# Weight slices 64 bytes further apart in SBUF, and x and g buffers at other distances modulo 512

## The chip, the cores and the metric

The kernel runs on one core of a Trainium2 chip. A core has a matrix engine (TensorE, PE in the profile, its weight loads PEld), a vector engine (VectorE, DVE), a scalar engine (ScalarE, ACT), GpSimd (POOL) and a queue engine (SyncE, SP) that issues the transfers (DMA) between main memory and the on-chip memory SBUF. SBUF has 128 partitions; an address below is a byte offset within a partition. TensorE reads both operands from SBUF (the weights, which it loads first, and the moving rows, which stream past them) and writes sums to PSUM. The metric is device time in microseconds, lower is better.

## What is computed

A linear attention with decaying state, and a feed-forward network on its output:

```python
for t in range(S):                       # S = 768, B, H, D = 4, 8, 48
    kt, vt, rt = (k[:, :, t], v[:, :, t], r[:, :, t])
    cur = np.einsum('bhd,bhe->bhde', u[None] * kt, vt)
    y[:, :, t] = np.einsum('bhd,bhde->bhe', rt, state + cur)
    state = w[None, :, :, None] * state + np.einsum('bhd,bhe->bhde', kt, vt)
x = np.ascontiguousarray(y.transpose(0, 2, 1, 3)).reshape(B * S, H * D)   # 3072 x 384
h = x @ w_in                             # 384 x 2048
g = h * np.clip(h + 3.0, 0.0, 6.0) / 6.0
return g @ w_out                         # 2048 x 384
```

All inputs and the output are float32.

## The kernel before

The attention is done in 24 half steps of 64 tokens (`attention`, small matmuls of L319). It leaves its output in the x buffers. The feed-forward network goes over 6 groups g of 512 tokens and, in each, over 16 slices f of 128 hidden units, 96 units in all. One unit is:

- `ffn1`: nine matmuls by `hidden` (L128) make h, 128 hidden units by 512 tokens. Three parts (weights high by x high, weights low by x high, weights high by x low: the table `PARTS`) times three blocks j of 128 rows of w_in. The high and low parts are a split of each float32 number in two, so that the fast matmul format (F32R) keeps enough digits.
- ACT takes relu(h + 3) to t (L388), DVE takes min(t, 6) times h (L390), ACT writes the high part of g (L394), DVE the low part (L183).
- `ffn2`: nine matmuls by `project` (L135) add g to three output sums o, with the same three parts times three blocks m.

Every one of the 18 matmuls has weights of its own, 128 x 128, taken from `w_hi` or `w_lo`, and moving rows of 512 elements, taken from x (L128) or g (L135). `ffn2` of a unit follows `ffn1` of the next one, so on TensorE groups of nine alternate: h of unit n+1, o of unit n, and so on. The order on every engine is made ahead of time: operations are recorded with estimated costs (class `Schedule`), a list scheduler sorts them, and the result is emitted as it stands. The estimates know sizes and engines, and no addresses.

During the first group of tokens the weights come in: `weights(f)` loads slice f of `wcat` into `raw[f % 2]` (L200), and ACT and DVE make from it `w_hi[:, f]` (L219 or L220) and `w_lo[:, f]` (L183). Where the schedule has TensorE idle, dummy matmuls on `ident` (L490) fill in.

The tiles that matter here, in the order in which they lie in SBUF: a reserve of 16384 bytes for descriptors of transfers that GpSimd issues (this kernel has none of those), four constants of 32 bytes, `w_hi` and `w_lo` of 16 slices each (one slice has 2 x 384 elements, 3072 bytes: w_in's part, then w_out's), the attention's tiles, x0 and x1 (16384 bytes each, used in turn by groups g), t0 and t1, g0, g1 and g2 (4096 bytes each, used in turn by units), `raw`, `z`, `cv`. A tile begins where the one before it ends. 3072, 4096, 16384 and 2048 (a t buffer) are multiples of 512, so all weight slices lie at one place modulo 512, and all x and g buffers at another.

Of the kernel before, what the change touches and what calls it, by code (L numbers as in the profile page):

```python
# [9 lines left out]
F32R = mybir.dt.float32r  # L10
# [12 lines left out]
DM, DFF = H * D, 2048  # L23
NF = DFF // 128
NG = NSTEP // 2

W_MIN, W_MAX = 0.5, 2.0

# [108 lines left out]
def fast_path(tc, mp, pp, sb, w_hi, w_lo, b3, wm, badi, hps, ops3, rT, kT, rt, kt, vt, wp, wu, wcat, out):  # L139
    nc = tc.nc  # L140
# [4 lines left out]
    def two(name, shape, dt=F32):  # L145
        return [sb(f"{name}{q}", shape, dt, mp) for q in range(2)]

    def one(name, shape, dt=F32):
        return sb(name, shape, dt, mp)
# [10 lines left out]
    PQ, IW = E[:, 0:8], E[:, 8:16, 1:C + 1]  # L160


    xt = two("x", [128, 2, 4, 2, 256], F32R)
    tt = two("t", [128, 512])
    gg = [one(f"g{q}", [128, 2, 512], F32R) for q in range(3)]
    mask = one("mask", [128, C], U8)
    NW = 2 * DM
    raw, z = two("raw", [128, NW], I64), two("z", [128, NW])
# [286 lines left out]
    for n, u in enumerate(units):  # L455
        g, f, c0, ns = u
# [26 lines left out]
    for (_, free, _, _), (start, _, _, _) in zip(pe, pe[1:]):  # L483
        n = int((start - free - 0.2) / 0.22)
# [14 lines left out]
def rwkv_ffn_kernel(ctx: ExitStack, tc: tile.TileContext, rT, kT, rt, kt, vt, wp, wu, wcat, ys, out):  # L499
    nc = tc.nc  # L500
# [3 lines left out]
    def sb(name, shape, dt=F32, pool=cp):  # L504
        return pool.tile(shape, dt, name=name)

    w_hi = sb("w_hi", [128, NF, 2, DM], F32R)
    w_lo = sb("w_lo", [128, NF, 2, DM], F32R)
    b3 = sb("b3", [128, 1])
    wm = sb("wm", [1, 4])  # L510
    badi = sb("badi", [1, 1], I32)
# [4 lines left out]
    with tc.tile_pool(name="main", bufs=1) as mp, tc.manual_schedule():  # L516
        fast_path(tc, mp, pp, sb, w_hi, w_lo, b3, wm, badi, hps, ops3, rT, kT, rt, kt, vt, wp, wu, wcat, out)
# [3 lines left out]
    with tc.If(bad != 0):  # L521
        with tc.tile_pool(name="fb", bufs=1) as fb, tc.tile_pool(name="fl", bufs=1) as fl:
# [11 lines left out]
            with tc.For_i(0, NSTEP, 1) as st:  # L534
                a = [fl.tile([128, C, D], F32, tag=f"a{n}", name=f"a{n}") for n in range(2)]
# [32 lines left out]
            with tc.For_i(0, NG, 1) as g:  # L568
                xf = fb.tile([128, 3, 512], F32, name="xf")
                x = fb.tile([128, 3, 2, 512], F32R, name="xr")  # L570
# [7 lines left out]
                for f in range(NF):  # L578
                    h, t, gt = hps[f % 2], fl.tile([128, 512], F32, tag="t", name="ft"), fl.tile(
                        [128, 2, 512], F32R, tag="gg", name="fg")  # L580
# [72 lines left out]
```

## Time and profile before

| | us |
|---|---|
| median of 3 runs | 521.6 |
| lowest and highest of them | 518.52, 525.86 |
| span of the profiled execution, first to last instruction | 520.5 |

The profile is of one execution of its own; its span is its time, and stands 1.1 us below the median of the three runs. Three stages can be seen in the table of stretches, whose columns are the length, each engine's busy time with its number of instructions, the granted clock of TensorE (1.00 is full), the share of the DMA engines and GB/s:

```profile
0.00:48.60 48.60, 43.20 (x842) 40.39 (x843) 40.00 (x64) 15.77 (x21) 17.93 (x22) 1.00 0.79 230
48.60:135.00 86.40, 81.83 (x1000) 64.83 (x1000) 78.32 (x106) 47.62 (x70) 23.93 (x17) 0.98 0.45 146
135.00:508.00 373.00, 372.68 (x3344) 301.28 (x3343) 178.05 (x279) 124.59 (x199) 38.11 (x35) 1.00 0.18 53
508.00:520.50 12.50, 3.96 (x22) 2.78 (x20) 1.38 (x2) 1.78 (x3) 0.00 (x0) 0.74 0.19 69
```

Up to 48.6 us the first half steps of the attention run and the first weights come in; up to 135 us the first 16 units run beside the rest of the weights; then come the other 80 units with the attention between them, and a tail of 12.5 us in which the last sums are written out. In the third row TensorE is busy for 372.68 of 373.00 us.

### The profile page before, as it was taken

To read this page: it belongs to the slowest core of one execution; us is meant where nothing else is said; L and a number is where in the kernel's file an instruction comes from. 1 tells how busy PE (TensorE), PEld (TensorE's weight loads), DVE (VectorE), ACT (ScalarE), POOL (GpSimd) and SP (SyncE) were. 2 spreads that over 40 slices of the span, in tenths; PEclk is the share of its full clock that TensorE was granted. 3 is DMA by queue.
4 is the path that set the end of the run, shared out by engine and by line. 5 is a ranking of instruction groups with operands and counts; after the bars stand their busy time and mean duration, and the time that the engine had idled before them with its cause. 6 is when DMAs were issued, how large, how long until landed. Compare 5 with 4: busy or idle time off the path is not lost.

```text
span 520.5 us, 11985 instructions
## 1 busy us (share of the span) xinstructions
PE 501.7 (96%) x5204; PEld 409.3 (79%) x5204; DVE 297.8 (57%) x449; ACT 189.8 (36%) x291; POOL 80.0 (15%) x73
## 2 busy tenths in 40 slices
PE   8799799999999999999999999999999999999993
PEld 8789587886888877888778888778888878888882
DVE  6899889979833477533576433577333463333331
ACT  1334667652433332333332333332433323333331
POOL 2253013244300122000231000231000220000000
PEclk9999899999999999999999999999999999999997
DMA  8976535452500153200254200253100110100001
GB/s 223 292 232 182 171 131 191 151 159 66 158 3 0 33 150 118 85 2 0 68 157 117 79 0 1 67 164 112 63 0 1 49 35 15 62 0 1 0 1 66
DMA packets 22909, 44.31 MB, mean 85 GB/s; under 512 B 3649, under 2 KB 11970, under 8 KB 22850
## 3 DMA queue, kind: packets, MB, share of 16 engines
q1 hardware_dynamic: 22850, 43.47, 27.3%
q8 instruction: 43, 0.70, 0.6%
q14 instruction: 16, 0.13, 0.1%
HBM read 36.38 MB, written 4.72 MB: 79 GB/s over the span
## 4 chain that ended last, share of the span: by engine, by line
PE 87%; DVE 5%; DMA 3%; SPq 1%; ACT 1%; issue 1%; DVEq 0%; ACTq 0%
PE o L135 38%; PE h L128 37%; PE PP L319 9%; DMA raw<-wcat 3%; PE h L490 2%; PE U L319 1%; DVE w_lo L183 1%; SPq L193 1%; DVE z L215 1%; DMA kt<-kt 1%; SPq L370 1%; DVE cv L213 1%; DVE z L183 0%; DVE g L183 0%; PE o L319 0%
## 5 line engine op out<-in xcount | busy, mean ns | idle before, releaser
L135 PE MATMUL o<-g,w_hi 128*128 128x512 f32 x576 | 199.3, 400 | 4.8 <-ACT g L394 3.2
L128 PE MATMUL h<-x,w_hi 128*128 128x512 f32 x576 | 165.2, 395 | 0.4 <-DVE w_hi L220 0.4
L390 DVE SCALAR_TENSOR_TENSOR t<-t,h 128x512 f32<-128x512 f32 x96 | 65.9, 686 | 132.3 <-ACT t L388 132.1
L135 PEld LDWEIGHTS o<-g,w_hi 128*128 128x128 f32 x576 | 108.6, 189 | 32.5 <-ACT g L394 3.7
L388 ACT ACTIVATE t<-h,b 128x512 f32<-128x512 f32 x96 | 66.1, 688 | 182.4 <-PE h L128 182.3
L128 PEld LDWEIGHTS h<-x,w_hi 128*128 128x128 f32 x576 | 106.7, 188 | 24.2 <-DVE w_hi L220 0.8
L135 PE MATMUL o<-g,w_lo 128*128 128x512 f32 x288 | 113.4, 394 | 0.0
L183 DVE TENSOR_TENSOR g<-t,g 128x512 fp32r<-128x512 f32 x96 | 70.2, 732 | 36.1 <-ACT g L394 35.9
L394 ACT CAST g<-t 128x512 fp32r<-128x512 f32 x96 | 59.5, 620 | 65.8 <-DVE t L390 65.8
L128 PE MATMUL h<-x,w_lo 128*128 128x512 f32 x288 | 81.7, 392 | 0.0
L128 PEld LDWEIGHTS h<-x,w_lo 128*128 128x128 f32 x288 | 54.0, 188 | 12.4 <-DVE w_lo L183 0.5
L135 PEld LDWEIGHTS o<-g,w_lo 128*128 128x128 f32 x288 | 54.4, 189 | 10.8
L183 POOL TENSOR_TENSOR ks<-kT,E 112x512 f32<-112x512 f32 x22 | 28.1, 1278 | 224.4 <-PE PP L319 163.3
L319 PE MATMUL U<-V,KH 64*48 64x48 f32 x704 | 40.0, 204 | 0.6 <-issue 0.6
L183 POOL TENSOR_TENSOR KH<-kt,TW 128x384 f32<-128x384 f32 x21 | 21.7, 1035 | 97.2 <-PE U L319 68.9
L319 PEld LDWEIGHTS U<-V,KH 64*48 64x48 f32 x704 | 34.5, 121 | 0.7 <-issue 0.7
L490 PE MATMUL h<-ident 128*128 128x128 f32 x236 | 29.2, 280 | 0.0
L490 PEld LDWEIGHTS h<-ident 128*128 128x128 f32 x236 | 27.6, 193 | 0.7
L319 PEld LDWEIGHTS PP<-X,V 64*48 64x48 f32 x736 | 18.1, 119 | 11.2 <-DVE X L351 4.2
L319 PEld LDWEIGHTS PP<-RP,ks 48*64 48x64 f32 x736 | 19.7, 132 | 7.6 <-issue 6.8
L319 PE MATMUL PP<-X,V 64*48 64x64 f32 x736 | 21.5, 227 | 3.4 <-DVE X L351 3.4
L362 ACT CAST x<-PP 112x512 fp32r<-112x512 f32 x23 | 13.5, 586 | 29.5 <-PE U L319 29.5
(77 smaller groups left out, 337.4 us busy)
## 6 DMA issues: line engine op xcount, KB each, us to landing
raw<-wcat SPq DMA_DIRECT2D x16, 768.0 KB, 4.7
kT<-kT SPq DMA_DIRECT2D x24, 224.0 KB, 3.0
rT<-rT SPq DMA_DIRECT2D x24, 224.0 KB, 3.4
kt<-kt SPq DMA_DIRECT2D x24, 192.0 KB, 3.0
V<-vt SPq DMA_DIRECT2D x24, 192.0 KB, 3.0
rt<-rt SPq DMA_DIRECT2D x16, 192.0 KB, 2.7
outT<-cv SPq DMA_DIRECT2D x12, 256.0 KB, 2.2
x<-x SPq DMA_DIRECT2D x72, 32.0 KB, 2.0
```

Source lines behind the costliest of these rows:

```text
L128: nc.tensor.matmul(h, (w_hi, w_lo)[wl][:, f, 0, 128 * j:128 * j + 128], x(j, hl), start=(m == 0 and j == 0), stop=(m == 2 and j == 2))
L135: nc.tensor.matmul(o[m], (w_hi, w_lo)[wl][:, f, 1, 128 * m:128 * m + 128], g(hl), start=(clear and k == 0), stop=(f == NF - 1 and k == 2), ...
L183: emit = lambda e: eng[e].tensor_tensor(out=out, in0=in0, in1=in1, op=op)
L193: S.add({"sp": cost}, [], [(name, q)], lambda e, dst=dst, src=src: dma(dst[q], src[i]), LEAD)
L213: S.add({"dve": 0.56}, [kr], [("cv", 1)], lambda e: dve.tensor_scalar(out=sg, in0=up_i, scalar1=-2 ** 31, scalar2=None, op0=ALU.bitwise_an ...
L215: S.add({"dve": 0.95}, [kz, ("cv", 1)], [kz], lambda e: dve.scalar_tensor_tensor(out=zi, in0=zi, scalar=3, in1=sg, op0=ALU.logical_shift_l ...
L319: nc.tensor.matmul(out, lhsT, rhs, start=start, stop=True, skip_group_check=True)
L362: S.add({"act": 0.59}, keys, [kx + (0,)], lambda e: act.copy(out=hi, in_=yt), LEAD)
L388: S.add({"act": 0.23 + 0.23 * ns}, [("h", n % 2), "b3"], [kt_], lambda e: act.activation(out=t[:, :T], in_=h[:, :T], func=AF.Relu, bias=b3 ...
L390: last = S.add({"dve": 0.13 + 0.28 * ns}, [("h", n % 2), kt_], [kt_], lambda e: dve.scalar_tensor_tensor(out=t[:, :T], in0=t[:, :T], scala ...
L394: S.add({"act": 0.18 + 0.22 * ns}, [kt_], [kg + (0,)], lambda e: act.copy(out=gt[:, 0, :T], in_=t[:, :T]))
L490: nc.tensor.matmul(hps[1][:, :128], ident, ident, start=True, stop=True)
```

## The change

The diff moves tiles in SBUF. On each engine the same instructions stand in the same order with the same shapes; only addresses differ.

```diff
+STEP = 16
+X_AT, G_AT = (0, 8), (0, 8, 4)
...
-    xt = two("x", [128, 2, 4, 2, 256], F32R)
+    def moved(name, n, at):
+        return one(name, [128, n + 8], F32R)[:, at:at + n]
+
+    xt = [moved(f"x{q}", 2 * 4 * 2 * 256, a).rearrange("p (c j l t) -> p c j l t", c=2, j=4, l=2)
+          for q, a in enumerate(X_AT)]
     tt = two("t", [128, 512])
-    gg = [one(f"g{q}", [128, 2, 512], F32R) for q in range(3)]
+    gg = [moved(f"g{q}", 2 * 512, a).rearrange("p (l t) -> p l t", l=2) for q, a in enumerate(G_AT)]
...
-    w_hi = sb("w_hi", [128, NF, 2, DM], F32R)
-    w_lo = sb("w_lo", [128, NF, 2, DM], F32R)
+    w_hi, w_lo = (sb(name, [128, NF, 2 * DM + STEP], F32R)[:, :, 0:2 * DM].rearrange("p f (a m) -> p f a m", a=2)
+                  for name in ("w_hi", "w_lo"))
...
-    nc = bacc.Bacc("TRN2", target_bir_lowering=False, num_devices=1)
+    nc = bacc.Bacc("TRN2", target_bir_lowering=False, num_devices=1, dynamic_dma_scratch_size=4096)
```

Each weight slice is followed by 16 unused elements (64 bytes), so slice f lies 64 f bytes further on. Each x and g buffer has 8 elements (32 bytes) more than it needs, and begins 0, 8 or 4 elements into its tile. The reserve at the start of SBUF shrinks from 16384 to 4096 bytes, which makes room. The addresses that follow:

| | bytes modulo 512, before | after |
|---|---|---|
| slice f of w_hi and of w_lo | 128 | (128 + 64 f) modulo 512 |
| x0, x1 | 192, 192 | 192, 256 |
| g0, g1, g2 | 192, 192, 192 | 256, 320, 336 |
| t0, t1 | 192, 192 | 256, 256 |
| raw0, raw1 (modulo 256) | 0, 0 | 160, 160 |

Before, the moving rows lie 64 bytes behind the weights, modulo 512, for every pair. After it, the distance is 64 - 64 f for x0, 128 - 64 f for x1 and g0, 192 - 64 f for g1 and 208 - 64 f for g2. So each buffer meets eight different distances as f goes from 0 to 15.

## The prediction, made before the changed kernel was run

> **What bounds the kernel now.** I read the page first: the span, the busy shares, the granted clock and the chain of work that ended last.
>
> ```profile
> span 520.5 us, 11985 instructions
> PE 501.7 (96%) x5204; PEld 409.3 (79%) x5204; DVE 297.8 (57%) x449; ACT 189.8 (36%) x291; POOL 80.0 (15%) x73
> PE 87%; DVE 5%; DMA 3%; SPq 1%; ACT 1%; issue 1%; DVEq 0%; ACTq 0%
> PE o L135 38%; PE h L128 37%; PE PP L319 9%; DMA raw<-wcat 3%; PE h L490 2%; PE U L319 1%; DVE w_lo L183 1%; SPq L193 1%; DVE z L215 1%; DMA kt<-kt 1%; SPq L370 1%; DVE cv L213 1%; DVE z L183 0%; DVE g L183 0%; PE o L319 0%
> ```
>
> TensorE is the bound, and by the chain's second line it is two lines of code: L128 (h from x and the weights) and L135 (o from g and the weights), 37% and 38%, together some 390 us of 520.5. The groups say how many instructions that is: 576 with `w_hi` and 288 with `w_lo` on each line, 1728 in all.
>
> ```profile
> L135 PE MATMUL o<-g,w_hi 128*128 128x512 f32 x576 | 199.3, 400 | 4.8 <-ACT g L394 3.2
> L128 PE MATMUL h<-x,w_hi 128*128 128x512 f32 x576 | 165.2, 395 | 0.4 <-DVE w_hi L220 0.4
> L135 PEld LDWEIGHTS o<-g,w_hi 128*128 128x128 f32 x576 | 108.6, 189 | 32.5 <-ACT g L394 3.7
> ```
>
> Their mean of 400 or 395 ns is not the pace, since matmuls overlap. The pace is read from the timeline in the last, undisturbed part (columns: start, length, engine, line, operands, count).
>
> ```profile
> 454.76 0.85 PE L128 MATMUL h<-x,w_hi 128*128 128x512 f32 x3
> 455.22 0.65 PEld L128 LDWEIGHTS h<-x,w_lo 128*128 128x128 f32 x3
> 455.45 0.85 PE L128 MATMUL h<-x,w_lo 128*128 128x512 f32 x3
> 456.13 0.85 PE L128 MATMUL h<-x,w_hi 128*128 128x512 f32 x3
> 457.05 0.39 PE L135 MATMUL o<-g,w_lo 128*128 128x512 f32 x1
> 457.05 0.42 PEld L135 LDWEIGHTS o<-g,w_hi 128*128 128x128 f32 x2
> 457.08 0.69 ACT L388 ACTIVATE t<-h,b 128x512 f32<-128x512 f32 x1 [2.06 <-PE h L128]
> 458.88 0.62 PE L128 MATMUL h<-x,w_hi 128*128 128x512 f32 x2
> 459.18 0.69 DVE L183 TENSOR_TENSOR g<-t,g 128x512 fp32r<-128x512 f32 x1 [0.69 <-ACT g L394]
> ```
>
> From 454.76 to 458.88 are 18 matmuls, nine of L128 and nine of L135: 4.12 us, 228.9 ns each, and 1728 x 228.9 = 395.5 us. That is the whole of the chain's 75% (390 us), so nearly every nanosecond won or lost per matmul counts in full. The rows show a second thing: each weight load starts with the matmul before the one that it serves (457.05 and 457.05). Two reads of SBUF by TensorE run side by side, and the change alters the distance between just these.
>
> **Is there something to win?** In one short stretch TensorE had half its clock.
>
> ```profile
> 57.30:59.60 2.30, 2.30 (x6) 1.82 (x7) 2.27 (x4) 1.69 (x3) 0.00 (x0) 0.50 0.08 12
> 58.31 0.63 PE L135 MATMUL o<-g,w_lo 128*128 128x512 f32 x1
> 58.74 1.05 PE L135 MATMUL o<-g,w_hi 128*128 128x512 f32 x2
> 59.59 0.56 PE L135 MATMUL o<-g,w_lo 128*128 128x512 f32 x1
> ```
>
> The first row is the table of stretches (its 0.50 is the granted clock). Three steps from 58.31 to 59.59 are 1.28 us, 427 ns each. Half of that, 213 ns, is what the same matmul would take at full clock if nothing else limited it. It takes 228.9. So some 15.6 ns of each matmul at full clock are not streaming, 1728 x 15.6 = 27 us in all. If these come from the weight load and the moving rows meeting in SBUF, the change can touch them: before, all weight slices lie at 128 modulo 512 bytes and all x and g buffers at 192, one distance (64) for every pair. After it, slices step through eight positions and the buffers lie at 192, 256, 256, 320 and 336.
>
> The trace has a test of that. Where the attention's matmuls follow, the last matmul of a group of L128 has no weight load beside it, because the next load comes late.
>
> ```profile
> 249.63 0.65 PEld L128 LDWEIGHTS h<-x,w_hi 128*128 128x128 f32 x3
> 249.86 0.85 PE L128 MATMUL h<-x,w_hi 128*128 128x512 f32 x3
> 250.64 0.21 PEld L319 LDWEIGHTS PP<-RP,ks 48*64 48x64 f32 x8 [0.36 <-issue]
> 250.81 0.69 ACT L388 ACTIVATE t<-h,b 128x512 f32<-128x512 f32 x1 [2.06 <-PE h L128]
> 245.74 0.85 PE L128 MATMUL h<-x,w_hi 128*128 128x512 f32 x3
> 246.20 0.19 PEld L135 LDWEIGHTS o<-g,w_hi 128*128 128x128 f32 x1
> 246.68 0.69 ACT L388 ACTIVATE t<-h,b 128x512 f32<-128x512 f32 x1 [2.05 <-PE h L128]
> ```
>
> In the upper four rows the third matmul starts at about 250.31 and the next weight load only at 250.64; in the lower three the load for L135 starts at 246.20 with the third matmul. ACT, which waits for that matmul, starts 0.95 us after the three began in the first case and 0.94 us in the second. Without a load beside it the matmul is not sooner done; if the load took 15 ns from it, the first figure would be the smaller. So the 15.6 ns are not shown to come from the load, and the distance between the two reads should not matter. Nor do other engines' accesses show: in the fence of 454.76 ACT and DVE read and write t and g during the run, and the 4.12 us hold.
>
> **The change, part by part.**
>
> *Weight slices 64 bytes further apart (L128, L135).* No instruction is added or moved. Per matmul the price is bounded by -15.6 ns (the row at half clock) and, upward, by a weight load that loses its cover:
>
> ```profile
> 108.07 0.50 PE L135 MATMUL o<-g,w_hi 128*128 128x512 f32 x1
> 108.17 0.19 PEld L135 LDWEIGHTS o<-g,w_lo 128*128 128x128 f32 x1
> 108.41 0.40 PE L135 MATMUL o<-g,w_lo 128*128 128x512 f32 x1
> ```
>
> Here the load came 0.10 us late and the next matmul started 0.34 us after the last instead of 0.23: +110 ns. Between -15.6 and +110 I take 0, since the nearest rows are those with and without a load, 0.94 and 0.95. What hides a somewhat slower load is the matmul beside it: a load takes 189 ns of the 229 (the mean in the groups' third row), so some 40 ns are free.
>
> *x and g at other offsets.* ACT and DVE write and read the same elements. The chain h, t, g that must be done before L135 starts on it: h ends at 456.98, ACT starts at 457.08, DVE's last step ends at 459.18 + 0.69 = 459.87, and the group of L135 that reads it comes after the nine matmuls from 458.88, at 458.88 + 2.06 = 460.94. So 1.07 us hide a slower write of g or x. I take 0. Were that cover gone, each further 0.1 us would cost 96 x 0.1 = 9.6 us; at four instructions of some 0.7 us it would take each of them over a third longer.
>
> *The reserve of 4096 instead of 16384 bytes, and all tiles after it.* No queue of GpSimd issues a transfer in this kernel, so the reserve itself costs nothing. But the tiles behind it shift: `raw` lay at a multiple of 256 bytes and now lies 160 past one (32 past a multiple of 64); kT, rT, V, kt and rt lie 32 past a multiple of 64 before and after. `raw` takes in the weights, and some of its landings are waited for:
>
> ```profile
> raw<-wcat SPq DMA_DIRECT2D x16, 768.0 KB, 4.7
> kT<-kT SPq DMA_DIRECT2D x24, 224.0 KB, 3.0
> L200 SPq DMA_DIRECT2D raw<-wcat x16: 327/328/1492, 5.1 to 103.3; - x16
> ACT z L210 <- DMA raw<-wcat: 5.2, 3, 2.5
> ACT cv L212 <- DMA raw<-wcat: 4.3, 1, 4.3
> DVE z L211 <- DMA raw<-wcat: 2.8, 1, 2.8
> ```
>
> Five waits, 12.3 us. Bounds: at best nothing changes; at worst `raw` moves at the rate of kT (224 KB in 3.0 us, 75 KB per us), 10.3 us instead of 4.7, which over five waits is +28 us. I take 0. The smaller transfer takes 3.0 us for under a third of the bytes, so most of a landing isn't bytes, and kT's rate is the size's doing far more than the position's.
>
> A rule of the Trainium skill speaks against the change here: "DMA: Bandwidth & Descriptors", section "How a descriptor splits into AXI transactions", says that a descriptor which doesn't start at a multiple of 256 bytes fetches from the boundary below. By it, as an estimate, a row of 6144 bytes at 160 past a boundary needs 197 beats instead of 192, 2.6% more, 0.12 us of 4.7, and the sum would have 0.6 us over five waits in place of 0. No run here shows which of the two ends of a transfer it concerns.
>
> **The sum.** Own time of the profiled execution 520.5 us; L128 and L135 0; ACT and DVE 0; DMA 0: 520.5. The median of the runs shown, 521.6, is 1.1 above that span, so the forecast is 521.6 us: no change. The runs shown of before differ among themselves by 7.3 us (518.52 to 525.86), and a measurement of this kernel can't tell less than about 2%, 10.4 us, from no change.
>
> **Rivals.**
>
> *The two reads do meet, and spreading them frees seven of eight pairs (faster).* For it speaks that the 15.6 ns are absent at half clock, where reads have twice the time; against it, that the matmul without a load beside it is as long. At 7/8 of 15.6 ns, 1728 matmuls give 23.6 us: 498 us. At half, 13.5 us: 508 us. It decides (10.4 us) from 6 ns per matmul. The Trainium skill ("TensorE: Matmul & The Clock Gate", section "Back-to-back issue gap") has N / 2.4 + 2.5 ns at full clock, 216 ns for 512 columns. By it, as an estimate, 1728 x 13 = 22.5 us would be there to win, 499 us; the trace shows 228.9 and no matmul at 216.
>
> *At one distance in eight a weight load loses its cover (slower).* Then 1728 / 8 = 216 matmuls pay 110 ns: +23.8 us, 546 us. It decides from 95 matmuls, one in 18, and needs a load over 40 ns longer than its 189. Against it: loads of both lines and both tables show 0.19 us everywhere at full clock. For it: only one distance was ever seen.
>
> *`raw` lands later (slower).* It decides when each of the five waited-for landings comes 2.1 us later, 6.8 instead of 4.7 us; at the upper bound the time is 550 us. Against it: it is 16 loads, the last issued at 103 us, and eleven of them land unwaited for.
>
> *The change does what it says and nothing comes of it* is the forecast itself.
>
> **How the numbers follow.** No change 0.78; the reads meet (faster by over 2%) 0.12; a load loses its cover 0.06; `raw` 0.04. Hence faster 0.12, same 0.78, slower 0.10. The likeliest case's own range is the spread of the runs with a microsecond on either side, 517 to 527. Reaching down to the half-size gain (508, with a microsecond for the spread: 507) and up to 528 leaves out the full gain, both slower cases and a tail: some 0.18.
>
> **What would show it.** Right: 18 matmuls still take 4.12 us in undisturbed stretches of every weight slice, for x0 and x1 and all three g, loads stay at 0.19, and `raw` lands in 4.7. The faster rival would show as a pace that changes with the slice, near 3.9 us per 18 for most and 4.12 for a few; the slower one as steps of 0.34 us at the same slices in every group, or as longer loads; the `raw` one as longer landings and longer waits before L210 to L212, all before 120 us. If the pace differs by slice at all, my reading of the matmul without a load beside it was wrong.

## The result: 0.6% slower, and a pace that now changes from slice to slice

The median of 20 runs is 526.05 us against 522.36 us before (20 runs). The ratio is 1.0064 with a 95% interval of 1.0042 to 1.0086: slower, by some 3.3 us. The ratio compares fast executions alone and leaves out two slow ones of the changed kernel (530.63 and 531.67 us), so it is a little smaller than that of the two medians. The loss is far inside the 2% that the forecast took for no change, but it is clear of zero, and the forecast had nothing that would cause it.

The page of the changed kernel hardly shows it (L132 is the old L128, L139 the old L135).

```profile
span 521.4 us, 11993 instructions
PE 504.3 (97%) x5204; PEld 409.1 (78%) x5204; DVE 297.6 (57%) x449; ACT 189.8 (36%) x291; POOL 82.0 (16%) x73
PE o L139 38%; PE h L132 38%; PE PP L327 8%; DMA raw<-wcat 2%; PE h L498 2%; PE U L327 1%; DMA kt<-kt 1%; DVE w_lo L191 1%; DVE z L223 1%; DVE z L191 1%; SPq L201 1%; DVE cv L221 1%; DVE X L359 1%; DVE g L191 0%; PE o L327 0%
L139 PE MATMUL o<-g,w_hi 128*128 128x512 f32 x576 | 199.3, 400 | 4.1 <-ACT g L402 2.3
L132 PE MATMUL h<-x,w_hi 128*128 128x512 f32 x576 | 166.4, 397 | 0.4 <-DVE w_hi L228 0.4
```

The chain is the same, TensorE is as busy, and the mean length of a matmul, 400 and 397 ns, is what it was to within 2 ns. The page's span is only 0.9 us longer, because one execution's start-up differs from the next by more than the effect: the first matmul of the second group of tokens begins at 132.96 us here and at 135.01 in the profile of before (131.8 to 140.7 over all the profiles below). The answer stands in the timeline. Two groups of nine matmuls of L132, from undisturbed stretches of the same page:

```profile
455.50 0.86 PE L132 MATMUL h<-x,w_hi 128*128 128x512 f32 x3
456.20 0.86 PE L132 MATMUL h<-x,w_lo 128*128 128x512 f32 x3
456.90 0.86 PE L132 MATMUL h<-x,w_hi 128*128 128x512 f32 x3
457.60 0.39 PE L139 MATMUL o<-g,w_hi 128*128 128x512 f32 x1
...
501.41 0.84 PE L132 MATMUL h<-x,w_hi 128*128 128x512 f32 x3
502.09 0.84 PE L132 MATMUL h<-x,w_lo 128*128 128x512 f32 x3
502.77 0.84 PE L132 MATMUL h<-x,w_hi 128*128 128x512 f32 x3
503.44 0.39 PE L139 MATMUL o<-g,w_hi 128*128 128x512 f32 x1
```

The first group (slice 3) takes 2.10 us for nine steps, 233 ns each; the second (slice 14) 2.03 us, 226 ns each. Before, an undisturbed group took 2.06. From the first matmul of L132 in unit 16 to that in unit 95 there are 372.54 us here and 369.19 before: +3.35 us, which is the loss. Of the 1422 steps from one matmul of the two lines to the next, 67 are over 260 ns long (the attention lies in between, or a group starts late) and take 58.90 us against 58.72 before. The other 1355, called undisturbed below, take 313.64 us against 310.47: +3.2 us, 2.3 ns each. So the loss is in the pace and not in the gaps.

From here on a pace is worked out from the starts of the matmuls in the trace: the mean of the last six of the eight steps within a group of nine, over all groups that no attention interrupts. Sorted by the distance of the moving rows from the weights, modulo 256 bytes, the changed kernel gives, for L132 and for L139 at the distances that are multiples of 64:

| distance | L132, ns | L139, ns |
|---|---|---|
| 0 | 229.0 (single groups 226.7 to 231.5) | 228.9 (227.3 to 231.5) |
| 64 (all pairs before: 228.9) | 229.3 (228.8 to 231.0) | 230.5 (228.8 to 233.3) |
| 128 | 232.7 | 232.8 |
| 192 | 233.3 | 233.3 |

The two buffers x0 and x1 meet a given distance at different slices and agree within 0.7 ns in the mean. Nothing of the rest of the change shows: `raw` lands in 4.6 us (4.7 before), and its waits are no longer than they were (4.9, 2.6 and 1.4 us against 5.2, 4.3 and 2.8).

```profile
raw<-wcat SPq DMA_DIRECT2D x16, 768.0 KB, 4.6
ACT z L218 <- DMA raw<-wcat: 4.9, 6, 1.3
ACT cv L220 <- DMA raw<-wcat: 2.6, 1, 2.6
DVE z L219 <- DMA raw<-wcat: 1.4, 1, 1.4
```

### The profile page after: what moved, and what is told of

Same layout as the page of the kernel before. It is cut to its first block, busy times and chain, and to the rows that moved or that the text cites. A ratio compares the mean times of both kernels' runs of the same rounds, so it can differ in the third digit from the quotient of the medians.

```text
span 521.4 us, 11993 instructions
## 1 busy us (share of the span) xinstructions
PE 504.3 (97%) x5204; PEld 409.1 (78%) x5204; DVE 297.6 (57%) x449; ACT 189.8 (36%) x291; POOL 82.0 (16%) x73
## 4 chain that ended last, share of the span: by engine, by line
PE 87%; DVE 6%; DMA 3%; ACT 1%; SPq 1%; issue 1%; DVEq 0%; ACTq 0%
PE o L139 38%; PE h L132 38%; PE PP L327 8%; DMA raw<-wcat 2%; PE h L498 2%; PE U L327 1%; DMA kt<-kt 1%; DVE w_lo L191 1%; DVE z L223 1%; DVE z L191 1%; SPq L201 1%; DVE cv L221 1%; DVE X L359 1%; DVE g L191 0%; PE o L327 0%
## 5 line engine op out<-in xcount | busy, mean ns | idle before, releaser
L139 PE MATMUL o<-g,w_hi 128*128 128x512 f32 x576 | 199.3, 400 | 4.1 <-ACT g L402 2.3
L132 PE MATMUL h<-x,w_hi 128*128 128x512 f32 x576 | 166.4, 397 | 0.4 <-DVE w_hi L228 0.4
L139 PEld LDWEIGHTS o<-g,w_hi 128*128 128x128 f32 x576 | 108.0, 188 | 32.3 <-ACT g L402 2.7
L132 PEld LDWEIGHTS h<-x,w_hi 128*128 128x128 f32 x576 | 106.8, 188 | 25.2 <-DVE w_hi L228 0.8
L139 PE MATMUL o<-g,w_lo 128*128 128x512 f32 x288 | 113.3, 393 | 0.0
L132 PE MATMUL h<-x,w_lo 128*128 128x512 f32 x288 | 82.2, 393 | 0.0
L132 PEld LDWEIGHTS h<-x,w_lo 128*128 128x128 f32 x288 | 54.0, 188 | 13.0 <-DVE w_lo L191 0.5
L139 PEld LDWEIGHTS o<-g,w_lo 128*128 128x128 f32 x288 | 54.2, 188 | 11.3
L191 POOL TENSOR_TENSOR KH<-kt,TW 128x384 f32<-128x384 f32 x21 | 23.9, 1140 | 97.6 <-PE U L327 70.2
```

Source lines behind the costliest of these rows:

```text
L132: nc.tensor.matmul(h, (w_hi, w_lo)[wl][:, f, 0, 128 * j:128 * j + 128], x(j, hl), start=(m == 0 and j == 0), stop=(m == 2 and j == 2))
L139: nc.tensor.matmul(o[m], (w_hi, w_lo)[wl][:, f, 1, 128 * m:128 * m + 128], g(hl), start=(clear and k == 0), stop=(f == NF - 1 and k == 2), ...
L191: emit = lambda e: eng[e].tensor_tensor(out=out, in0=in0, in1=in1, op=op)
```

## The experiments

The theory after the result: the pace of a matmul follows the distance, modulo 256 bytes, between its moving rows and the weights, and the old kernel happened to sit at one of the better distances. Rivals: the places themselves count (of slices, or of buffers), the intake of the weights does (`raw`, `z`, `cv` moved too), or the pace is a matter of what ran before.

All kernels below start from the kernel before, with the small reserve. Their helpers pad with whole multiples of 512 bytes, so that everything that isn't named keeps its place modulo 512. The edit that they share, offsets in elements of 4 bytes:

```diff
-    xt = two("x", [128, 2, 4, 2, 256], F32R)
+    def moved(name, n, at):
+        return one(name, [128, n + -(-at // 128) * 128], F32R)[:, at:at + n]
...
-    w_hi = sb("w_hi", [128, NF, 2, DM], F32R)
-    w_lo = sb("w_lo", [128, NF, 2, DM], F32R)
+    def slices(name, at):
+        n = NF * (2 * DM + STEP)
+        w = sb(name, [128, -(-(at + n) // 128) * 128], F32R)[:, at:at + n].rearrange("p (f k) -> p f k", f=NF)
+        return w[:, :, 0:2 * DM].rearrange("p f (a m) -> p f a m", a=2)
+
+    w_hi, w_lo = (slices(name, at) for name, at in zip(("w_hi", "w_lo"), W_AT))
```

### The three parts of the change, one at a time

The slices alone:

```diff
+STEP, W_AT = 16, (0, 0)
+X_AT, G_AT = (0, 0), (0, 0, 0)
```

> Weight slices 64 bytes further apart as in the change; x, g, raw and all other tiles at the places modulo 512 that they had before. Distance theory (the pace of a matmul follows the distance modulo 256 bytes between its moving rows and the weights, 229 ns at 0 and 64, 233 at 128 and 192): slices f = 0, 1, 4, 5, ... at about 229 ns, the others at about 233, mean 231, 1728 x 2.2 = 3.8 us more than before, ratio 1.007. Rival, places of the buffers (the new places of x and g cost it): 228.9 ns everywhere, ratio 1.000. Rival, intake (raw, z and cv at other places cost it): ratio 1.000, since these are back.

Measured: 525.3 us, ratio 1.0067 (1.0022 to 1.0112). At distances 128 and 192 the pace is 232.3 to 233.3 ns in every group, at 0 it is between 226.7 and 231.3, at 64 between 228.8 and 233.3. The slices alone cost what the change costs, with the buffers and `raw` in their old places.

The spread at 64 is not noise. From unit 16 on, o (L137 here) averages 229.4 ns at this distance, but h (L130) takes 233.3 in 15 of its 20 groups. It takes 229 only in unit 16 and in the four groups that come directly behind the attention's matmuls. A group of h and one of o of the same slice, both at 64, from an undisturbed stretch (2.10 us and 2.06 us for nine steps):

```profile
462.25 0.86 PE L130 MATMUL h<-x,w_hi 128*128 128x512 f32 x3
464.35 0.39 PE L137 MATMUL o<-g,w_hi 128*128 128x512 f32 x1
...
468.52 0.39 PE L137 MATMUL o<-g,w_hi 128*128 128x512 f32 x1
470.58 0.86 PE L130 MATMUL h<-x,w_hi 128*128 128x512 f32 x3
```

In the kernel before and in the changed one h holds 229 at 64. So the distance does not fix the pace alone, and the expected mean of 231 ns came out near (231.7 over the undisturbed steps) although one of its terms was wrong.

The buffers alone:

```diff
+STEP, W_AT = 0, (0, 0)
+X_AT, G_AT = (0, 16), (16, 32, 36)
```

> The x and g buffers at the places modulo 512 that the change gives them (192, 256; 256, 320, 336), slices, raw and the rest as before. Distances 64 and 128 for x, 128, 192 and 208 for g. Distance theory: 228.9 ns for x0, 232.7 for x1 and g0, 233.3 for g1, 231 to 233 for g2, 231.7 in the mean, 1728 x 2.8 = 4.9 us more, ratio 1.009: more than the whole change. Rival, the two parts of the change add up to its 1.0064 and the slices alone had 1.0067: ratio 1.000.

Measured: 526.19 us, ratio 1.0086 (1.0048 to 1.0124), with 229.4 ns for x0, 232.8 for x1, 232.4 for g0, 233.3 for g1 and 232.5 for g2. So either part alone costs as much as both. They are not two costs that add up: each sends pairs away from one good distance, and from there it makes little difference how. With the first run this rules out the places of the slices and of the buffers taken by themselves.

The shift of `raw`, `z` and `cv` alone (a gap of 160 bytes ahead of `raw`):

```diff
+    one("gap", [128, 40])
     raw, z = two("raw", [128, NW], I64), two("z", [128, NW])
```

> The third part of the change alone: the small reserve, and raw, z and cv 160 bytes past a multiple of 256 as the change has them; slices and buffers at the old distance of 64. Distance theory: 228.9 ns everywhere, ratio 1.000. Rival, intake: raw lands later than 4.7 us and the ratio is 1.003 or more.

Measured: 523.54 us, ratio 1.0008 (0.9967 to 1.0050); 228.9 ns everywhere, and `raw` lands in 4.5 us. With the old pace kept, the intake does not explain the loss of the change, which lies behind the last load (unit 16 to unit 95).

### The distance, evenly bad and evenly good

Every pair at 192 bytes, by moving the buffers:

```diff
+STEP, W_AT = 0, (0, 0)
+X_AT, G_AT = (32, 32), (32, 32, 32)
```

> Weight slices as before, every x and g buffer moved so that it lies 192 bytes behind the weights, modulo 512, in place of 64. Distance theory: 233.3 ns in all groups, 1728 x 4.4 = 7.6 us more, ratio 1.015, twice the loss of the change. Rival, places of the slices: they are where they were, so 228.9 ns and ratio 1.000. Rival, intake: ratio 1.000.

Measured: 527.81 us, ratio 1.0114 (1.0075 to 1.0153), somewhat under the 1.015 that was expected, which the interval still reaches. The pace is 233.3 ns in every group, as its timeline shows (L130 and L137 are the two lines here): 4.20 us from 455.21 to 459.41, for 18.

```profile
455.21 0.39 PE L137 MATMUL o<-g,w_hi 128*128 128x512 f32 x1
457.30 0.86 PE L130 MATMUL h<-x,w_hi 128*128 128x512 f32 x3
459.41 0.39 PE L137 MATMUL o<-g,w_hi 128*128 128x512 f32 x1
```

A finer look at the distances in a single kernel, by slices that are 16 bytes further apart:

```diff
+STEP, W_AT = 4, (0, 0)
+X_AT, G_AT = (0, 0), (0, 0, 0)
```

> Weight slices 16 bytes further apart, buffers at their old place: distances 64, 48, 32, 16, 0, -16, ... -176 bytes for f = 0 to 15, the same for x and g. Distance theory: the pace goes with f and is the same for x0, x1 and all g: near 229 ns at f = 0 and 4, near 233 at f = 8 (-64) and f = 12 (-128), and the curve between is what this run is for; a distance with under 228 ns in every group would be a better place than that of before. Rival, time (the pace depends on what ran before, not on the distance): no order by f.

One run (524.62 us). The pace in ns, the mean of five or six groups for each entry:

| distance | 0 | 16 | 32 | 48 | 64 | 80 | 96 | 112 | 128 | 144 | 160 | 176 | 192 | 208 | 224 | 240 |
|---|---|---|---|---|---|---|---|---|---|---|---|---|---|---|---|---|
| h (x) | 227.4 | 227.1 | 233.2 | 232.6 | 229.0 | 230.5 | 233.3 | 233.6 | 233.0 | 233.1 | 234.4 | 231.8 | 234.0 | 233.3 | 233.3 | 226.7 |
| o (g) | 226.7 | 226.6 | 233.2 | 232.9 | 228.9 | 229.2 | 233.3 | 233.6 | 232.8 | 233.0 | 234.0 | 231.9 | 233.3 | 233.3 | 233.3 | 233.3 |

Two good windows, at 0 and 16 and, less good, at 64 and 80; nearly everything else is at 233. The old kernel's 64 lay in the second. The two lines agree but at 240, where h has 226.7 and o 233.3 in all six groups each: two paces at one distance, which says again that distance is not all. The order by slice is clear all the same: the rival that only what ran before counts is not borne out.

In steps of 4 bytes:

```diff
+STEP, W_AT = 1, (7, 7)
+X_AT, G_AT = (0, 0), (0, 0, 0)
```

> Weight slices 4 bytes further apart and all 28 bytes further on: distances 36, 32, 28, ... down to -24 bytes for f = 0 to 15. Distance theory in steps of 16 bytes: 226.7 ns where the distance is from 0 to 16 (f = 5 to 9), 233 at 32 and at -16, with an edge between that tells how wide the good window is. Rival, only whole multiples of 16 bytes are good: 233 or more at all distances but 0 and 16.

One run (526.52 us). There is no window from 0 to 16: h takes 228.3 ns at 0, 233.3 at 4, 8 and 12, 228.2 at 16, 231 from 20 to 28 and 233.4 at 32. (o agrees to 0.5 ns, except 229.7 at 0 and, between 226.7 and 233.3, 228.9 at 4.) The rival, whole multiples of 16 bytes, describes it better, but is not right either: it expected 233 or more at all other distances, and 20 to 28 take 231 ns, -8 and -12 230.5 to 230.8. At -16, which is 240 modulo 256, both lines are at 233.3, where h had 226.7 in the run before. In this kernel the weights themselves begin off multiples of 16 in three slices of four, so whether it is their distance or their own place that counts here isn't told apart.

Every pair at 16 bytes, then at 0, by moving the slices:

```diff
+STEP, W_AT = 0, (12, 12)
+X_AT, G_AT = (0, 0), (0, 0, 0)
```

> All weight slices 48 bytes further on modulo 512, evenly, so that every x and g buffer lies 16 bytes behind the weights instead of 64; all else at the old places. Distance theory: 226.7 ns in all groups as at 16 bytes in the run with slices 16 bytes apart, 1728 x 2.2 = 3.8 us less than before, ratio 0.993. Rival, history (226.7 came only because the slice before it had another distance; kept for good, the pace settles elsewhere, as it was 226.7 or 231 at distance 0): between 229 and 231, ratio 1.000 to 1.007.

Measured: 519.26 us, ratio 0.9937 (0.9902 to 0.9971): faster than the kernel before and than the changed one. 18 matmuls take 4.08 us, 226.7 ns each:

```profile
455.63 0.84 PE L130 MATMUL h<-x,w_hi 128*128 128x512 f32 x3
457.67 0.39 PE L137 MATMUL o<-g,w_hi 128*128 128x512 f32 x1
459.71 0.62 PE L130 MATMUL h<-x,w_hi 128*128 128x512 f32 x2
```

After an interruption some groups run at 228 to 231 before it settles, in one stretch for some eight units in a row (up to unit 55).

```diff
+STEP, W_AT = 0, (16, 16)
+X_AT, G_AT = (0, 0), (0, 0, 0)
```

> All weight slices 64 bytes further on, evenly: distance 0 for every pair. At this distance earlier runs had 226.7 ns in some groups and 230 to 231 in others. If the pace depends on the distance alone, with a mean of some 229: ratio 1.000. If one of the two holds once it is reached: 226.7 ns throughout, ratio 0.993, or 230.5 throughout, ratio 1.005.

Measured: 520.17 us, ratio 0.9925 (0.9888 to 0.9962). Most groups run at 226.7, some after the attention at 228.5 to 232.5, and the last part (units 82 to 94) at 226.7 throughout. So at distance 0 there are two paces, the better one holds once it is reached, and interruptions can leave it. The changed kernel, which came to distance 0 anew from another distance each time, caught it in a part of the groups only.

The mean of the undisturbed steps from unit 16 to unit 95 orders the four kernels that have one distance for all pairs: 233.3 ns at 192, 229.1 at 64, 227.3 at 16 and 227.7 at 0. The ratios to the kernel before follow it (1.0114, 1, 0.9937 and 0.9925), but for the last two, whose intervals overlap.

### Which weights: a matmul's own, or those loaded beside it?

`w_lo` moved by 128 bytes against `w_hi`:

```diff
+STEP, W_AT = 0, (0, 32)
+X_AT, G_AT = (0, 0), (0, 0, 0)
```

> w_lo 128 bytes further on modulo 512, all else at the old places, so that x and g lie 64 bytes behind w_hi and 192 before w_lo. Theory that the moving rows meet the next weights, which are loaded beside them: of the three steps of L135 for one m, that from the first matmul (its rows run while w_lo loads) is the long one. Theory that a matmul's own weights matter: that from the second (own weights w_lo) is the long one. Both: 229 ns for the other steps, about 233 for the long one, some 230.3 in the mean.

One run (524.52 us), and no answer: nearly all steps of o are at 233 ns (one at 238, one at 226), though two of three of its matmuls are at the good distance from their own weights. In h, where the parts come three by three, either theory has three long steps, the third to the fifth or the fourth to the sixth; there is one clearly long step, the fourth (235 ns), and it lies in both.

In each slice w_out's part first, w_in's 16 bytes further on:

```diff
 PARTS = ((0, 0), (1, 0), (0, 1))
+OUT, IN = 0, 1
+STEP, W_AT = 64, (8, 8)
...
+        return w[:, :, 0:2 * DM + 8].rearrange("p f (a m) -> p f a m", a=2)[:, :, :, 0:DM]
...
-    wcat = np.concatenate([wi, wo], axis=2).view(np.int64)
+    wcat = np.concatenate([wo, wi], axis=2).view(np.int64)
```

> In each slice w_out's part comes first and w_in's 16 bytes further on modulo 256: x lies 16 bytes behind its own weights (w_in) and 32 behind w_out, g lies 32 behind its own (w_out) and 16 behind w_in. Inside a group 226.7 ns for L128 and 233.3 for L135 by both theories. The last matmul of each group tells them apart, since the weights loaded beside it are those of the other line. Theory that the weights loaded beside a matmul count: the step from L128 to L135 takes 233 and that from L135 to L128 takes 227. Theory that a matmul's own weights count: 227 and 233.

One run (521.24 us). Inside the groups 228.2 ns for h and 233.4 for o. Both steps between the lines are mostly short: h to o 228.4 in the mean, o to h 230.1 (most at 228, some at 237). The first step inside each group is out of place too: 235 in h, where the others are 226 to 230, and 229 in o, where they are 231 to 235. Neither theory says so, and a step's length seems to show one or two matmuls late. The question stays undecided.

A steady pattern is better than a single step. The next four kernels start from the one with all pairs at 16 bytes; they multiply other columns than the reference's, so they serve for the pace alone. Every second matmul takes weights and rows 32 bytes further on, so that each matmul's own distance is 16 and that to the weights loaded beside it -16 or 48:

```diff
+ROWS, WTS = (0, 8), (0, 8)
...
-            nc.tensor.matmul(h, (w_hi, w_lo)[wl][:, f, 0, 128 * j:128 * j + 128], x(j, hl),
+            odd = (3 * m + j) % 2
+            w = 128 * j + WTS[odd]
+            b = 512 * j + 256 * hl - 512 * (m == 2 and j == 2) + ROWS[odd]
+            nc.tensor.matmul(h, (w_hi, w_lo)[wl][:, f, w:w + 128], x[:, :, b:b + 256],
```

> Every second matmul of L128 and L135 takes weights that begin 32 bytes further on and moving rows that begin 32 bytes further on, so that each matmul's rows lie 16 bytes behind its own weights, and -16 or 48 bytes behind the weights that are loaded beside it. What is multiplied is thereby other columns than the reference's. Theory that a matmul's own weights count: 226.7 ns everywhere, some 519 us. Theory that the weights loaded beside it count: about 233 ns, some 528 us. Both count: 233.

Measured: 531.42 us in one run, 230.0 ns in some groups and 233.3 in others. The time says little of the pace, since the second group of tokens begins at 140.7 us in its profile, 5.7 us later than before; from unit 16 to unit 95 it takes 373.02 us.

```diff
-ROWS, WTS = (0, 8), (0, 8)
+ROWS, WTS = (8, 0), (0, 8)
```

> The mirror image: the other matmuls take the rows 32 bytes further on, so that each matmul's rows lie 16 bytes behind the weights loaded beside it and 48 or -16 behind its own; again other columns than the reference's are multiplied. Theory of a matmul's own weights: 233 ns, some 528 us. Theory of the weights loaded beside it: 226.7 ns everywhere, some 519 us. Both count: 233.

Measured: 523.39 us in one run, 228.3 ns for h and 231.0 for o. This fits none of the three theories (a matmul's own weights count, those loaded beside it, or both): neither kernel came to 226.7, and they are not both at 233. Here the weights that were to be at the bad distance have two distances in turn, so the same pair was run with 128 bytes, where they have one:

```diff
-ROWS, WTS = (0, 8), (0, 8)
+ROWS, WTS = (0, 32), (0, 32)
```

> As the pair before, with 128 in place of 32 bytes, so that one distance stands everywhere: each matmul's rows lie 16 bytes behind its own weights and 144 behind those loaded beside it. Other columns than the reference's are multiplied. Theory of a matmul's own weights: 226.7 ns, some 519 us. Theory of the weights loaded beside it: 233 ns as at 144 before, some 528 us.

```diff
-ROWS, WTS = (0, 32), (0, 32)
+ROWS, WTS = (32, 0), (0, 32)
```

> The mirror image: rows lie 16 bytes behind the weights loaded beside the matmul and 144 behind its own; other columns than the reference's are multiplied. Theory of a matmul's own weights: 233 ns, some 528 us. Theory of the weights loaded beside it: 226.7 ns, some 519 us. If the two runs of the pair come out alike, neither theory holds.

Measured, one run each: 522.95 and 524.63 us, and a pace that is the same in both, 230.0 ns. The timelines, first of the kernel with 16 bytes to a matmul's own weights, then of its mirror image:

```profile
455.43 0.85 PE L134 MATMUL h<-x,w_hi 128*128 128x512 f32 x3
457.50 0.39 PE L144 MATMUL o<-g,w_hi 128*128 128x512 f32 x1
459.56 0.62 PE L134 MATMUL h<-x,w_hi 128*128 128x512 f32 x2
```

```profile
455.02 0.39 PE L144 MATMUL o<-g,w_hi 128*128 128x512 f32 x1
457.09 0.85 PE L134 MATMUL h<-x,w_hi 128*128 128x512 f32 x3
459.16 0.39 PE L144 MATMUL o<-g,w_hi 128*128 128x512 f32 x1
```

18 matmuls take 4.13 and 4.14 us by the rounded starts; inside the groups nearly all eight steps of the trace are 230 ns. That is just half way from 226.7 (all distances 16) to 233.3 (the pace of most bad distances). Neither theory holds alone; it looks as if each role costs 3.3 ns where its distance is bad. But in this pair consecutive rows also lie 128 bytes apart, which no other kernel here has, and so do consecutive weights (else only with `w_lo` moved), so that reading stays a reading.

## Why the prediction was wrong

- *What bounds the kernel, and that each nanosecond per matmul counts:* right. The undisturbed steps are 2.3 ns longer, which makes 3.2 of the 3.35 us, and no order, wait or transfer is needed to explain it.
- *"So the 15.6 ns are not shown to come from the load, and the distance between the two reads should not matter":* this is the step that failed, and with it the term "L128 and L135 0" of the sum, which measured +3.2 us from unit 16 to unit 95. The first half may stand; the second doesn't follow from it. The test compared 0.95 and 0.94 us, figures rounded to 10 ns, at the one distance that the kernel had. It could have shown a loss of 15 ns to the load, and not one of 2 to 5. In the kernel with all pairs at 192 bytes, whose pace is worse (233.3 ns), the same reading is as silent: there the ninth matmul of a group of h signals its end 407.5 ns after its start in the mean without a load beside it and 408.8 with one; in the kernel before these are 409.3 and 405.7. What the runs showed in place of the step is that moving only the slices (1.0067) or only the buffers (1.0086) costs as much as the change. Through which part of TensorE or SBUF the places act stays open.
- *"Between -15.6 and +110 I take 0":* the price was +2.3 ns in the mean of all distances, by the sign the other way from what the half-clock row suggested. The ends were far too wide to be of use, and what was wanted was missing: the old kernel had shown one distance of sixteen, so that nothing told whether it was a good or a bad one. It was a good one.
- *The rival that spreading frees seven of eight pairs:* that position matters was right, and its sign was wrong, since the old distance was among the good ones; that the two reads meet is not shown. By the section "Back-to-back issue gap" of the Trainium skill's "TensorE: Matmul & The Clock Gate", 22.5 us were an estimate of what there is to win; no run reached 216 ns as the pace of a group, and the best pace, 226.7, is worth some 3 us.
- *A weight load that loses its cover:* no. From unit 16 on, steps of some 0.34 us come at the same 36 places in both profiles, always as the first step of a group: behind the attention's matmuls, and in the first group of o for each group of tokens. Loads stay at 0.19 us.
- *`raw` later, and the reserve:* right to take 0; alone it measures 1.0008 with an interval that holds 1. The 0.6 us, an estimate by the Trainium skill's "DMA: Bandwidth & Descriptors", section "How a descriptor splits into AXI transactions", is smaller than that interval, so no run here shows it.
- *"a measurement of this kernel can't tell less than about 2%, 10.4 us, from no change":* too coarse. With 20 runs on either side the interval is 0.44% wide, and a loss of 0.6% stood clear of it.
- *"If the pace differs by slice at all, my reading of the matmul without a load beside it was wrong":* that is what came.

## What to carry to other kernels

Where one kind of instruction makes up three quarters of the span, its operands' addresses are a parameter of the kernel: here the distance between weights and moving rows, modulo 256 bytes, is worth from -0.7% to +1.1%, and whoever shifts a tile for another reason can pay or win that without seeing why. A probe is cheap: let the distance grow by 16 bytes from slice to slice, and one profile has a curve. It gives candidates only, since the same distance can have another pace in another order of slices (64 for h in the kernel with the slices alone). Then put every pair at the best distance, instead of spreading them, and time that kernel. And a comparison that finds no difference says only that it is smaller than what the rows can resolve.

## What the runs showed of the hardware that was not expected

- Matmuls with 512 moving elements in this format run mostly at one of a few paces: 226.7, 228.9, 230.0, 231 or 233.3 ns from start to start at full clock, where half the time at half clock is 213. Which one depends on the two operands' places: where all pairs have one distance, modulo 256 bytes, mostly 226.7 at 0 and 16, 228.9 at 64, 233.3 at 192. In the kernel with slices 16 bytes further apart, most other distances are at about 233.
- At some distances there are two paces: 226.7 and 230 to 231.5 at 0, 229 and 233.3 at 64, 226.7 and 233.3 at 240. One can hold for many groups until something interrupts it. What makes the choice was not found.
- The remaining 13 ns between 226.7 and 213 were not moved by any kernel here, and whether they have to do with the weight loads is open.
